# Bucketed attention and two MLPs on one core: the product with v of the first batch goes behind the scores of six steps later

## The chip, the cores and the metric

One core of a Trainium2 chip runs the whole program in one launch. The metric is the device time of one execution in microseconds. Each kernel is timed several times and the median is given. The engines named below are PE (TensorE, matmuls; PEld is its weight load), DVE (VectorE), ACT (ScalarE), POOL (GpSimd) and SP (SyncE, whose queue issues nearly all DMAs here).

## What is computed

Attention over 2 batches of 8 heads, 768 positions, head dimension 64. A query sees only the keys with the same six sign bits. Then two MLPs (512 to 2048 to 512) run over the 1536 rows of 512.

```python
q_bits = (np.einsum('bhsd,dk->bhsk', q, proj) > 0)   # the same for k; bucket = the six bits as a number
scores = np.where(q_bucket[:, :, :, None] == k_bucket[:, :, None, :], scale * q @ k.T, -1e9)
attn = softmax(scores)                                # exp(scores - max), divided by the sum + 1e-9
x = (attn @ v).transpose(0, 2, 1, 3).reshape(1536, 512)
x = gelu_like(x @ w_in1, 1.702) @ w_out1              # h * sigmoid(1.702 h)
out = gelu_like(x @ w_in2, 1.0) @ w_out2              # h * sigmoid(h)
```

## The kernel before

The attention is cut into 96 steps of 128 query rows: six steps a head, 48 steps (steps 0 to 47) a batch. The heads go in pairs. A step j runs through these functions, each with its own line and engine:

- `scores(j)`: four matmuls on PE (lines 404 and 405, twice each) into one of two PSUM buffers `pss`. The second of each pair adds the mask of the buckets.
- `top(j)`: DVE takes the minimum over the row and copies the scores to SBUF tile `p` (line 422). This frees the PSUM buffer, so scores j+2 wait for top j.
- `exps(j)`: ACT, line 427. `p_high(j)`: the f16 half of p into `hl` (line 436 on DVE or 438 on ACT). `p_low(j)`: POOL subtracts it from p, the rest is the lower f16 half (line 442).
- `p_turn(j)`, at odd j: one DMA transpose on SP (line 448) turns the `hl` of two steps into `pt`. There are two `pt` buffers (`PTB = 2`), each for a pair of steps. So the transpose of the pair m (steps 2m and 2m+1) waits until PE is through with the `pt` of pair m-2.
- `av(j)`: 18 matmuls on PE (lines 460 to 462) multiply `pt` by v into the PSUM tile `pav`. It needs the landed transpose.
- `norm`, after the last step of a head's group: DVE divides by the row sums (lines 472 to 476); after the second head of a pair PE transposes the result (line 488, tile `psx`) and ACT and DVE split it into XH and XL (lines 494, 495), which the first MLP reads.

Beside the steps, `ahead` prepares the next pair of heads: loads of q, k and v on SP (lines 268, 279), splits on DVE and POOL (292, 293), transposes on PE (line 300, tile `pstr`), evictions on ACT (307), moves and mask rows by DMA on SP (316, 347), bits on PE (332).

The loop at line 559 runs batch 0 (steps 0 to 47) and then batch 1. In batch 0 an iteration i traces scores i+2, av i-LAG with LAG = 3, top i+1, norm, ahead, exps i, p_high, p_low and p_turn i-1. In batch 1 the scores are one step ahead instead of two, and chunks of the first MLP are traced between the steps. From the iteration `SWITCH - 1` on, which is the last of the first batch's loop, the MLP's PSUM pool takes the place of the scores' second buffer.

The traced order is not the order on the engines. When the program is built, a planner simulates it and puts each engine's instructions in a fixed order: whenever an engine is free in the simulation, it takes the ready instruction with the lowest priority number, which is the place in the trace less an offset (`SOONER`, by function; in batch 0 `av` and `scores` have none, `norm` has 35, all of `ahead` 100 and its functions more). On the chip each engine then works strictly in that order and waits at an instruction whose semaphores aren't there yet. `tc.issue_after(x)` binds the instructions traced inside it to a place behind x in their engine's order; it adds no semaphore.

Of the kernel before, what the change touches and what calls it, by code (L numbers as in the profile page):

```python
# [21 lines left out]
def tile_lsh_attention_two_mlps(  # L22
# [13 lines left out]
    V, A, G, T, SP = nc.vector, nc.scalar, nc.gpsimd, nc.tensor, nc.sync  # L36

    B, H, S, D = q.shape
# [4 lines left out]
    NC = S // P  # L43
    HS = S // 2
    HC = NC // 2
    HEADS = B * H
# [13 lines left out]
    QSCALE = -1.0 / math.sqrt(D)  # L60
    assert math.frexp(QSCALE)[0] == -0.5
    NBUF = 3
    LAG = 3
    TUL = 1
    MORE = {'aq': 1, 'ak': 1, 'p': 1, 'hl': 1, 'pt': 0}
    PTB = 2
# [12 lines left out]

    SOONER = ({'ahead': 100, 'move': 20, 'load_v': 400, 'evict': 200, 'p_high': 200, 'natural': 800, 'p_turn': 35, 'turn': 100, 'p_low': 75, 'top': 35, 'exps': 75, 'bits': 300, 'norm': 35, 'load': 50, 'signs': 20}, {'scores': 200, 'evict': 50, 'norm': 300, 'av': 400, 'natural': 200, 'gate': 50, 'p_turn': 20, 'load_v': 200, 'load': 20, 'sum': 150, 'move': 20, 'p_high': 150, 'rows': 100, 'p_low': 75, 'bits': 100, 'exps': 20}, {'gate': 300, 'sum': 10, 'weights': 50})  # L80
    RATE = (3.4, 2.85)
    SWITCH = HEADS // 2 * NC + LAG + 1
    RING = 3
    RING2 = 6

# [2 lines left out]
    def sooner(task):  # L88
        n = SOONER[stage[0]].get(task, 0)
        return tc.high_priority(offset=n) if n else nullcontext()  # L90
# [158 lines left out]
    def attention(sp, s1, ps_m, ps_v, ahead_of, setup):  # L249
        nat, st = {}, {}  # L250
# [12 lines left out]
        N = len(steps)  # L263
# [55 lines left out]
        def place(n):  # L319
            return n % (NBUF + 1) if n < H else (n - H) % NBUF  # L320
# [74 lines left out]
        def scores(j):  # L395
            n, c = steps[j]
            aq, ak = st["q", n], st["k", n]
            bq, bk = BQ[place(n)], BK[place(n)]
            ps = ahead_of["pool"].tile([P, 2, 512], F32, tag="s", name="pss")
            lq = aq.rearrange("p a b -> p (a b)")[:, c * P:(c + 1) * P]  # L400
            bq = bq[:, c * P:(c + 1) * P]
            for half in range(2):
                o = ps[:, half, 0:HS]
                T.matmul(o, lhsT=lq, rhs=ak[:, half, :], start=True, stop=False)  # L404
                T.matmul(o, lhsT=bq, rhs=bk[:, half * HS:(half + 1) * HS], start=False, stop=True)  # L405
            st["S", j] = ps[:, :, 0:HS]

        count = {}
# [42 lines left out]
        def av(j):  # L451
            (n, c), g = steps[j], group[j]
            vs, s = st["v", n // 2]
            pt = st.pop(("pt", j))
            if j == g[0]:
                st["av", g] = ps_v.tile([P, 512], F32, tag="av", name="pav")
            o = st["av", g][:, c * (D + 1):(c + 1) * (D + 1)]
            for i in range(NC):
                hv, lv = vs[:, n % 2, i, 0:D + 1], vs[:, n % 2, i, D + 1:]
                T.matmul(o, lhsT=pt[:, i], rhs=hv, start=(i == 0), stop=False)  # L460
                T.matmul(o[:, 0:D], lhsT=pt[:, i], rhs=lv, start=False, stop=False)
                T.matmul(o, lhsT=pt[:, NC + i], rhs=hv, start=False, stop=(i == NC - 1))


        def norm(g):
            n, c0 = steps[g[0]]
            m = len(g)
            pr, j = divmod(n, 2)
            vs, s = st["v", pr]
            y = st.pop(("av", g))[:, 0:NC * (D + 1)].rearrange("p (c d) -> p c d", c=NC)[:, c0:c0 + m]  # L470
            ri = sp.tile([P, NC, 1], F32, tag="ri", name="ri", bufs=1)[:, 0:m]
            V.tensor_scalar(ri, y[:, :, D:D + 1], EPS, s[:, j:j + 1], op0=ALU.add, op1=ALU.mult)
            V.reciprocal(ri, ri)
            if ("x", pr) not in st:
                st["x", pr] = sp.tile([P, NC, 2, D], F32, tag="xn", name="xn", bufs=1)
            V.tensor_tensor(out=st["x", pr][:, c0:c0 + m, j, :], in0=y[:, :, 0:D],
                            in1=ri.to_broadcast([P, m, D]), op=ALU.mult)
            if j == 1:
                halves = range(c0 // HC, (c0 + m) // HC)
                for half in halves:  # L480
                    x_turn(pr, half)
                for half in halves:
                    x_split(pr, half)
# [14 lines left out]
        def ahead(pr, s):  # L498
            a, b = 2 * pr, 2 * pr + 1
            return {  # L500
                -4: [(natural, a, "k")],
                -3: [(turn, a, "k", 0), (load, b, "k")],
                -2: [(evict, a, "k", 0), (turn, a, "k", 1), (natural, a, "q")],
                -1: [(evict, a, "k", 1), (turn, a, "q", 0), (v_max, pr), (load, b, "q")],
                0: [(evict, a, "q", 0), (turn, a, "q", 1), (natural, b, "k"), (move, a, "k")],
                1: [(evict, a, "q", 1), (turn, b, "k", 0), (load, a + 2, "k")],
                2: [(turn, b, "k", 1), (v_spread, pr), (natural, b, "q"), (move, a, "q")],
                3: [(evict, b, "k", 0), (evict, b, "k", 1), (turn, b, "q", 0), (v_scale, pr), (load, a + 2, "q")],
                4: [(evict, b, "q", 0), (turn, b, "q", 1), (v_high, pr, 0), (move, b, "k")],
                5: [(evict, b, "q", 1), (bits, pr, 0), (v_low, pr, 0)],  # L510
                6: [(signs, pr, 0), (bits, pr, 1), (v_high, pr, 1), (move, b, "q")],
                7: [(signs, pr, 1), (rows, pr), (v_low, pr, 1)],
                8: [(load_v, pr + 1)],
            }.get(s, [])

        def run(fs):
            for f, *a in fs:
                with sooner(f.__name__):
                    f(*a)
# [36 lines left out]
            run(ahead(1, s))  # L556


        for lead, first, last in ((2, 0, N // 2), (1, N // 2, N)):
            def at(f, j):  # L560
                if first <= j < last:
                    with sooner(f.__name__):
                        f(j)

            for i in range(first - lead, last + LAG + 1):
                if lead == 2:
                    at(scores, i + 2)
                at(av, i - LAG)
                at(top, i + lead - 1)
                m = i - LAG  # L570
                if first <= m < last and m == group[m][-1]:
                    with sooner("norm"):
                        norm(group[m])
                m = i - 2 * (2 - lead)
                if first <= m < last:
                    pr, s = divmod(m, 2 * NC)
                    with sooner("ahead"):
                        if pr + 1 < HEADS // 2:
                            run(ahead(pr + 1, s))
                        if s >= 2 * NC - 4 and pr + 2 < HEADS // 2:  # L580
                            run(ahead(pr + 2, s - 2 * NC))
                at(exps, i)
                at(p_high, i)
                at(p_low, i)
                at(p_turn, i - TUL)
                yield i
                if lead == 1:
                    at(scores, i + 1)
# [107 lines left out]
    with ExitStack() as es:  # L696
# [9 lines left out]
        for i in attention(sp, s1, ps_m, ps_v, ahead_of, lambda: attention_setup(sp, s1, am, ps_m)):  # L706
            if i == -2:
                for _ in range(EARLY):
                    W.fetch()
            if gen is None and i >= WSTART and i % WEVERY == 0 and W.done < 4:  # L710
                W.step()
            if gen is None and i == SWITCH - 1:
                ps_s.close()
                stage[0] = 1
                ahead_of["lead"] = 1
                ahead_of["more"] = {}
                mb = es.enter_context(tc.tile_pool(name="mlpb", bufs=2))
                ahead_of["pool"] = es.enter_context(tc.tile_pool(name="ps_s1", bufs=1, space=PSUM))
                ps_h = es.enter_context(tc.tile_pool(name="ps_h", bufs=2, space=PSUM))
                gen = mlp(0, [0, 1], [[f, f + 1] for f in range(0, NF, 2)], W, mb, ps_h, True, first1)  # L720
            if gen is not None:
                credit += RATE[i >= 3 * HEADS // 4 * NC]
                while credit >= 1.0:
                    credit -= 1.0
                    next(gen, None)
                    background()
# [41 lines left out]
```

## Time and profile before

| | us |
|---|---|
| median of 3 runs | 835.03 |
| lowest and highest run | 831.97 and 836.65 |
| the profiled execution | 831.93 |
| its span, first to last instruction | 830.1 |
| PE busy (91% of the span) | 753.3 |
| DVE, POOL, ACT busy | 533.9, 442.0, 421.4 |

The times below are from the profiled execution, counted from the start of its span. The first batch's steps run from about 9 us (first scores) to 173 us (last product with v), the second batch's, mixed with the first MLP over the first batch's rows, up to about 415 us, and the rest is the MLPs alone. An idle engine costs nothing by itself. What counts in a stretch is the engine or queue whose waits end last.

### The profile page before, as it was taken

What the parts mean: (1) busy time and instruction counts of PE and PEld (TensorE: products, weight loads), DVE (VectorE), ACT (ScalarE), POOL (GpSimd) and SP (SyncE); (2) the same over time, 40 slices, a digit from 0 to 9 for tenths busy, and PEclk for the clock granted to TensorE, in tenths of its full rate; (3) what the DMA queues carried; (4) which work ended last, traced back from release to release, by engine and by line L of the source; (5) the groups of instructions that cost most, each with busy time, mean ns of one, the idle gap of its engine ahead of it and who ended that gap; (6) DMA issues with size and microseconds to landing.
All of it is one profiled execution on the core that took longest, in us unless ns stands there. A gap on an engine that the chain in (4) does not pass through costs nothing.

```text
span 830.1 us, 13998 instructions
## 1 busy us (share of the span) xinstructions
PE 753.3 (91%) x5384; PEld 692.9 (83%) x5384; DVE 533.9 (64%) x932; ACT 421.4 (51%) x721; POOL 442.0 (53%) x345
## 2 busy tenths in 40 slices
PE   6787787698898998988999999979999999999998
PEld 5677576577797887887999999979999989998996
DVE  8877787988689889779424233899733843422222
ACT  6758656596675666655534232444645433321220
POOL 5656676777777857766733242549534533421120
PEclk9778979599999999999999999999999999999999
DMA  4999999998998979865587421232310400000112
GB/s 117 190 180 193 200 180 223 231 247 238 246 254 231 223 216 226 210 153 109 108 300 261 150 104 49 77 127 95 108 51 21 132 2 1 0 1 1 39 39 76
DMA packets 196270, 116.40 MB, mean 140 GB/s; under 512 B 153318, under 2 KB 175846, under 8 KB 196204
## 3 DMA queue, kind: packets, MB, share of 16 engines
q1 hardware_dynamic: 196044, 115.52, 55.8%
q8 instruction: 42, 0.69, 0.3%
q14 instruction: 24, 0.20, 0.1%
q10 hardware_dynamic: 160, 0.00, 0.0%
HBM read 56.63 MB, written 16.78 MB: 88 GB/s over the span
## 4 chain that ended last, share of the span: by engine, by line
PE 59%; DVE 20%; DMA 10%; ACT 5%; issue 4%; POOL 1%; SPq 1%; DVEq 0%; ACTq 0%; POOLq 0%
PE pso L642 26%; PE psh L608 25%; DMA pt<-hl 6%; DVE f L173 3%; DVE p L422 3%; DVE f L171 3%; DVE f L175 2%; DVE f L172 2%; PE pss L404 2%; PE pss L405 1%; PE psbit L332 1%; POOL hl L442 1%; DMA nk<-in_k_dram 1%; PE pav L460 1%; ACT p L427 1%
## 5 line engine op out<-in xcount | busy, mean ns | idle before, releaser
L619 POOL TENSOR_TENSOR gl<-g,gh 128x384 fp32r<-128x384 f32 x128 | 138.3, 1081 | 201.7 <-ACT gh L618 189.5
L442 POOL TENSOR_TENSOR hl<-p,hl 128x768 f16<-128x768 f32 x96 | 168.0, 1757 | 75.7 <-ACT hl L438 33.2
L608 PE MATMUL psh<-XH,wih 128*128 128x384 f32 x512 | 174.2, 340 | 6.0 <-DVE part L651 3.9
L608 PE MATMUL psh<-XH,wil 128*128 128x384 f32 x512 | 173.0, 338 | 0.0
L608 PE MATMUL psh<-XL,wih 128*128 128x384 f32 x512 | 172.9, 338 | 0.0
L617 DVE TENSOR_TENSOR g<-g,psh 128x384 f32<-128x384 f32 x96 | 52.7, 550 | 116.8 <-ACT g L616 116.7
L651 DVE SCALAR_TENSOR_TENSOR part<-pso,part 128x384 f32<-128x384 f32 (+1 forms) x124 | 72.6, 590 | 83.0 <-PE pso L642 82.8
L427 ACT ACTIVATE p<-p,lo 128x768 f32<-128x768 f32 x96 | 89.7, 937 | 70.4 <-DVE p L422 70.2
L618 ACT CAST gh<-g 128x384 fp32r<-128x384 f32 x128 | 65.5, 512 | 86.7 <-DVE g L617 70.7
L608 PEld LDWEIGHTS psh<-XH,wih 128*128 128x128 f32 x512 | 97.2, 190 | 8.1 <-DVE g L614 2.2
L642 PE MATMUL pso<-gh,woh 128*128 128x384 f32 x256 | 88.6, 352 | 16.9 <-DVE g L614 7.0
L422 DVE TENSOR_SCALAR_CACHE_REDUCE p<-pss 128x768 f32<-128x768 f32 x96 | 90.8, 947 | 14.9 <-PE pss L405 8.6
L608 PEld LDWEIGHTS psh<-XL,wih 128*128 128x128 f32 x512 | 97.2, 190 | 0.6
L608 PEld LDWEIGHTS psh<-XH,wil 128*128 128x128 f32 x512 | 97.2, 190 | 0.0
L616 ACT ACTIVATE g<-psh 128x384 f32<-128x384 f32 x96 | 46.8, 488 | 96.2 <-PE psh L608 95.2
L404 PE MATMUL pss<-ak,aq 128*128 128x384 f32 x192 | 77.4, 404 | 19.7 <-DVE p L422 19.5
L642 PE MATMUL pso<-gl,woh 128*128 128x384 f32 x256 | 86.5, 338 | 0.0
L642 PE MATMUL pso<-gh,wol 128*128 128x384 f32 x256 | 86.5, 338 | 0.0
L460 PE MATMUL pav<-VS,pt 128*128 128x65 f16 x576 | 69.4, 205 | 15.4 <-DMA pt<-hl 13.0
L460 PEld LDWEIGHTS <-pt 128*128 128x128 f16 x576 | 57.4, 105 | 24.1 <-DMA pt<-hl 17.7
L642 PE MATMUL pso<-woh,gh 128*128 128x512 f32 x192 | 74.9, 390 | 0.2 <-ACT gh L618 0.2
L642 PE MATMUL pso<-wol,gh 128*128 128x512 f32 x192 | 75.0, 391 | 0.0
(114 smaller groups left out, 1623.1 us busy)
## 6 DMA issues: line engine op xcount, KB each, us to landing
raw<-in_moe_w_in_dram SPq DMA_DIRECT2D x32, 512.0 KB
raw<-in_moe_w_out_dram SPq DMA_DIRECT2D x32, 512.0 KB
spih<-wih SPq DMA_DIRECT2D x13, 256.0 KB
spil<-wil SPq DMA_DIRECT2D x13, 256.0 KB
spoh<-woh SPq DMA_DIRECT2D x13, 256.0 KB
spol<-wol SPq DMA_DIRECT2D x13, 256.0 KB
wih<-spih SPq DMA_DIRECT2D x13, 256.0 KB
wil<-spil SPq DMA_DIRECT2D x13, 256.0 KB
```

The source lines that it names most:

```text
L404: T.matmul(o, lhsT=lq, rhs=ak[:, half, :], start=True, stop=False)
L422: V.tensor_scalar(p, st.pop(("S", j)), LOW, None, op0=ALU.min, op1=ALU.min, accum_out=lo)
L427: A.activation(p, p, AF.Exp, bias=lo, scale=-1.0)
L442: G.tensor_tensor(out=hl[:, 1], in0=st.pop(("p", j))[0], in1=hl[:, 0], op=ALU.subtract)
L460: T.matmul(o, lhsT=pt[:, i], rhs=hv, start=(i == 0), stop=False)
L608: T.matmul(h, lhsT=a[:, c], rhs=x[t][:, c], start=(n == 0), stop=(n == 3 * NDC - 1))
L616: A.activation(g, h, AF.Sigmoid, scale=beta)
L617: V.tensor_tensor(out=g, in0=g, in1=h, op=ALU.mult)
L618: A.copy(gh[:, f], g)
L619: G.tensor_tensor(out=gl[:, f], in0=g, in1=gh[:, f].bitcast(F32), op=ALU.subtract)
L642: T.matmul(y, lhsT=a, rhs=x, start=(n == 0), stop=(n == 3 * nf - 1))
L651: V.scalar_tensor_tensor(out=acc, in0=y, scalar=scale, in1=acc, op0=ALU.mult, op1=ALU.add)
```

## The change

`LAG` becomes a pair, 4 for the first batch and 3 for the second, so that in batch 0 `av(j)` and the norm behind it are traced one iteration later. `SWITCH` moves with it by one, and so stays at the last iteration of the first batch's loop. `scores` keeps its last matmul under `st["did", j]`. In batch 0 the 18 matmuls of `av(j)` are traced inside `tc.issue_after` of the last matmul of scores j+6. Steps 42 to 47 have no scores j+6 yet when they are traced, and are not bound; nor is batch 1.

```diff
-    LAG = 3
+    LAGS = (4, 3)
...
-    SWITCH = HEADS // 2 * NC + LAG + 1
+    SWITCH = HEADS // 2 * NC + LAGS[0] + 1
...
-                T.matmul(o, lhsT=bq, rhs=bk[:, half * HS:(half + 1) * HS], start=False, stop=True)
+                st["did", j] = T.matmul(o, lhsT=bq, rhs=bk[:, half * HS:(half + 1) * HS], start=False, stop=True).ins
...
-            for i in range(NC):
-                hv, lv = vs[:, n % 2, i, 0:D + 1], vs[:, n % 2, i, D + 1:]
-                T.matmul(o, lhsT=pt[:, i], rhs=hv, start=(i == 0), stop=False)
-                T.matmul(o[:, 0:D], lhsT=pt[:, i], rhs=lv, start=False, stop=False)
-                T.matmul(o, lhsT=pt[:, NC + i], rhs=hv, start=False, stop=(i == NC - 1))
+            first = st.get(("did", j + 6)) if j < N // 2 else None
+            with tc.issue_after(first) if first is not None else nullcontext():
+                for i in range(NC):
+                    hv, lv = vs[:, n % 2, i, 0:D + 1], vs[:, n % 2, i, D + 1:]
+                    T.matmul(o, lhsT=pt[:, i], rhs=hv, start=(i == 0), stop=False)
+                    T.matmul(o[:, 0:D], lhsT=pt[:, i], rhs=lv, start=False, stop=False)
+                    T.matmul(o, lhsT=pt[:, NC + i], rhs=hv, start=False, stop=(i == NC - 1))
...
-        for lead, first, last in ((2, 0, N // 2), (1, N // 2, N)):
+        for lead, first, last, LAG in ((2, 0, N // 2, LAGS[0]), (1, N // 2, N, LAGS[1])):
```

## Rows read from the trace of the kernel before

**Rows 1.** Windows by stage: length, busy time of each engine (instructions), PE clock, DMA share.

```profile
20.00:44.00 24.00, 16.89 (x162) 14.85 (x163) 18.91 (x35) 16.48 (x25) 15.24 (x11) 0.74 0.92 188
44.00:154.00 110.00, 86.87 (x974) 74.88 (x971) 89.78 (x167) 74.75 (x108) 71.23 (x45) 0.84 1.01 195
168.00:415.00 247.00, 219.90 (x1934) 201.54 (x1933) 202.34 (x352) 161.48 (x267) 173.08 (x124) 0.97 0.85 205
```

**Rows 2.** SP's issues by line, 65.8 to 132.9 us: ns minimum/median/maximum, first and last start.

```profile
L448 SPq DMA_TRANSPOSE pt<-hl x12: 3580/4179/4519, 65.8 to 128.6; - x12
L347 SPq DMA_DIRECT2D BK<-mk x4: 743/796/852, 70.7 to 106.6; - x4
L347 SPq DMA_DIRECT2D BQ<-mk x4: 743/768/887, 71.6 to 107.3; - x4
L268 SPq DMA_DIRECT2D nq<-in_q_dram x4: 328/516/518, 74.1 to 118.2; - x4
L268 SPq DMA_DIRECT2D nk<-in_k_dram x3: 573/576/576, 78.8 to 113.5; - x3
L279 SPq DMA_DIRECT2D nv<-in_v_dram x2: 385/454/523, 70.1 to 104.4; - x2
L316 SPq DMA_DIRECT2D BQ<-aq x4: 523/592/596, 89.0 to 132.2; - x4
```

**Rows 3.** SP's waits, 44 to 154 us: in total, times, longest.

```profile
SPq L448 <- POOL hl L442: 49.5, 18, 3.8
...
SPq L268 <- DVE sq L293: 2.2, 1, 2.2
...
SPq L448 <- PE pav L462: 0.6, 2, 0.3
```

**Rows 4.** SP's timeline around 50 us and from 109 us: start, duration, issue.

```profile
50.40 0.33 SPq L268 DMA_DIRECT2D nq<-in_q_dram  x1
...
109.00 4.48 SPq L448 DMA_TRANSPOSE pt<-hl  x1
...
114.21 3.89 SPq L448 DMA_TRANSPOSE pt<-hl  x1
...
118.89 4.21 SPq L448 DMA_TRANSPOSE pt<-hl  x1
```

**Rows 5.** POOL's `p_low` counted to 109.05 us: ns minimum/median/maximum, first and last start.

```profile
L442 POOL TENSOR_TENSOR hl<-p,hl x32: 1641/1658/1972, 17.1 to 107.4; 128x768 f16<-128x768 f32 x32
```

**Rows 6.** PE's waits, 20 to 160 us: in total, times, longest.

```profile
PE pss L404 <- DVE p L422: 13.9, 15, 3.4
PE pav L460 <- DMA pt<-hl: 9.6, 6, 3.6
```

**Rows 7.** PE's last matmuls of scores and of av, counted to 42.71 and to 140.63 us.

```profile
L405 PE MATMUL pss<-BK,BQ x22: 336/340/648, 11.8 to 38.5; 128*128 128x384 f32 x22
L462 PE MATMUL pav<-VS,pt x24: 191/192/246, 30.0 to 37.6; 128*128 128x65 f16 x24
...
L405 PE MATMUL pss<-BK,BQ x92: 333/338/648, 11.8 to 136.1; 128*128 128x384 f32 x92
L462 PE MATMUL pav<-VS,pt x228: 190/193/278, 30.0 to 137.7; 128*128 128x65 f16 x114
```

**Rows 8.** PE's timeline at two waits before av: start, duration, [idle before <-releaser].

```profile
42.72 0.24 PE L460 MATMUL pav<-VS,pt 128*128 128x65 f16 x1 [3.64 <-DMA pt<-hl]
...
45.12 0.67 PE L404 MATMUL pss<-ak,aq 128*128 128x384 f32 x1
...
47.02 0.52 PE L404 MATMUL pss<-ak,aq 128*128 128x384 f32 x1
...
115.40 0.20 PE L460 MATMUL pav<-VS,pt 128*128 128x65 f16 x1 [1.70 <-DMA pt<-hl]
...
116.77 0.19 PE L462 MATMUL pav<-VS,pt 128*128 128x65 f16 x1
```

**Rows 9.** ACT's and DVE's timelines behind the wait at 42.72 us.

```profile
44.72 0.49 ACT L307 ACTIVATE aq<-pstr 128x384 fp32r<-128x384 f32 x1 [3.44 <-PE pstr L300]
...
44.95 0.95 DVE L364 TENSOR_REDUCE am<-nv 128x2 f32<-128x768 f32 x1 [4.21 <-DMA nv<-in_v_dram]
```

## The prediction

> **What bounds the kernel now.** I read four views in this order. The windows by stage come first, to find what is scarce in the first batch, the only place that the change binds. From 44 to 154 us no compute engine is full: DVE is busy 89.78 of 110 us, PE 86.87, ACT 74.75, POOL 71.23, while the DMA share is 1.01 [rows 1]. In the second batch PE has 219.90 of 247 us and the DMA share falls to 0.85.
>
> Then SP's issues, because all of that DMA traffic is issued by one queue. Between the transpose at 65.84 and the one at 132.98, 67.1 us in which two pairs of heads (12 pairs of steps) go by, SP issues 12 transposes of 4.18 us, 8 mask rows of 0.78, 4 + 3 loads of q and k of 0.52 and 0.58, 2 loads of v of 0.45 and 4 moves of 0.59: 50.2 + 6.3 + 2.1 + 1.7 + 0.9 + 2.4 = 63.6 us [rows 2]. So SP is 95% occupied and the pace of a pair of steps, 67.1 / 12 = 5.6 us, is SP's pace.
>
> Third, whether the 4.18 us hide a wait. The view of SP's waits gives 49.5 us to POOL's p_low [rows 3], and this is not to be believed: POOL had finished 32 p_lows (steps 0 to 31) by 109.1 us [rows 5], so both steps of pair 15 were there, and its transpose at 114.21 still took 3.89 us [rows 4]. The view names a later count of the same semaphore. The length is the issue itself. What is left of real waiting on SP from 44 to 154 us is 2.2 us once for a split of q, and 0.6 us in two waits for PE's av, which holds the `pt` buffer [rows 3].
>
> Fourth, PE's waits. Before av PE waits 9.6 us in six places for a landing transpose, and 13.9 us before scores for top [rows 6]. These are the waits that the change can touch. They lie on an engine that has 23 us to spare in that stretch.
>
> **The change part by part.** The sum is made against the profiled execution, 831.93 us (span 830.1 and 1.8 around it). The median of the runs is 835.03, 3.1 above it, and the forecast is moved by that.
>
> *The edge.* It adds no instruction and no semaphore, only an order. 42 steps get it. Does it bind? By 42.71 us PE has run 22 / 2 = 11 scores (0 to 10) and 24 / 6 = 4 avs; the next is av 4, behind scores 10, which is j+6 already. By 140.63 us it has run 46 scores (0 to 45) and 38 avs, so av 38 stands behind scores j+7 [rows 7]. Steady state fulfils the edge as it is. One step that doesn't is av 5, which runs on to 45.1 us, with scores 11 right after it [rows 8]. There scores 11 go ahead. They take about 1.9 us (45.12 to 47.02), so av 5 ends that much later; the next user of its buffer is the transpose behind 50.40 us on SP [rows 4], so this is hidden with 3 us to spare, and would cost 1.9 without that cover. Scores 11 come up to 1.4 us earlier. Bounds -1.4 to +1.9; I take 0, since the transpose behind 50 us is the next thing that could be late.
>
> *One iteration later in the trace.* `av` has no offset, so its number rises by what an iteration traces. It changes the order only where av and other work are ready at the same time in the planner's simulation: transposes of the next heads, x_turn, a score. Each such swap puts work into one of the six waits. At most all 9.6 us go and lie on the path; at least nothing. Where did such a wait reach SP? The longest, 3.64 us before 42.72 [rows 8], held back a transpose for ACT, which idled 3.44 us to 44.72; but DVE in that time idled 4.21 us for the load of v, to 44.95 [rows 9], and the split of q that SP then waits 2.2 us for is DVE's. So PE's wait was 0.2 us from being covered by DVE's. I take -0.5, nearest to that row, with -9.6 as the far end. If the wait goes, next late is the load of v for DVE, and behind it SP itself.
>
> *Later av holds `pt` longer.* What is queued behind a late av on PE is scores, and behind the `pt` buffer SP's whole queue, loads and mask rows too. The transpose at 109.00 was landed and used at 115.40, 6.40 us on, and the two avs took to 116.96, 1.56 us [rows 4, 8]. The transpose after next, which needs that buffer, was issued at 118.89: 1.93 us to spare. Below that a later av costs 0; bounds 0 and +7 (worked out in the third rival); I take 0, because the order that av has now already satisfies the edge. A rule of the Trainium skill speaks against the change at this point: "Perfetto Trace Analysis", section "Optimization Strategy", says that the same gap repeating on an engine can mean too few buffers for the next tile. The two `pt` buffers would then be what PE's gaps come from, and holding them longer would make it worse; by that rule the sum would be the third rival's, by the row of 1.93 us to spare it stays at 0.
>
> *The norm one iteration later, SWITCH, second batch.* The switch stays at the loop's last iteration, so nothing is added there. The norm is short DVE work behind av. The rest of the plan is remade: PE idles 27.1 us of 247 in the second batch [rows 1], and I allow a tenth of it in both directions, 2.7 us, with 0 taken.
>
> Sum: 831.93 + 0 - 0.5 + 0 + 0 = 831.4, on the median 834.5 us.
>
> **The rivals.**
> - *The waits before av are worth their length.* Scores and transposes slip into them, tops start sooner, and SP gets its hl and free buffers earlier. For it: six waits, 9.6 us, and a clock of 0.84 in that stretch, a mean over its two levels (1.2 and 2.4 GHz). Against it: SP has only 67.1 - 63.6 = 3.5 us in 67 free. Whole: 835.0 - 9.6 = 825.4; half: 830.2.
> - *It does nothing.* All edges but one are fulfilled and the planner chooses as before: 835.0.
> - *SP comes to wait for PE.* Place: the wait ahead of each transpose for the av of the pair before last, now 0.6 us in total. If av moves behind one more step of work, 5.6 / 2 = 2.8 us, it passes the 1.93 us by 0.87 for every second transpose. Per pair of heads four of six transposes follow without mask rows between them: 1.7 us, over four pairs 7 us: 842. The point from which it decides is a delay of 1.93 us behind the landing.
>
> **How the numbers follow.** About 0.5%, 4.2 us, is what a measurement of this kernel tells from no change: faster is below 830.9, slower above 839.2. Forecast and "does nothing" lie in between: 0.27 and 0.14, together 0.41; the forecast's own range is 831 to 839. The waits paid back, from half of them to all: 0.34, since the row of SP speaks against more than that but the new plan of the second batch can add its 2.7. SP waiting: 0.25. The range of 825 to 842 reaches to the whole of both rivals and leaves out some 2 in 10.
>
> **What would show it.** In the changed kernel's profile: SP's issues from 65 to 133 us still about 63 us of the same 67; SP's wait for av under 2 us in all (the third rival: over 5); PE's waits before av for the landing shorter than 9.6 us, and that time turning up as waits before scores; av 5 behind scores 11, the others behind j+7 or j+8. The last av of step 47 should end within 2 us of 173 us. Wrong it would be if the first batch ends more than 4 us earlier or later, or if it ends the same and the second batch moves.

## The result, and the profile after

The changed kernel takes 840.84 us in the median of 6 runs (836.71 to 842.67), the kernel before 834.70 in 6 runs beside it (831.97 to 836.65). The ratio (over the runs; it is not simply that of the two medians) is 1.0067, with a 95% interval of 1.0042 to 1.0093, so the change costs 0.4 to 0.9%. A second series, with its own runs of the kernel before, gave 1.0101 [1.0068, 1.0133]. The profiled execution of the changed kernel took 840.05 us with a span of 838.3, against 831.93 and 830.1 before: 8.2 us of span to explain. The line numbers of the changed kernel are one higher up to `p_turn` (449), and four higher from `av`'s matmuls (464 to 466) on.

Begin with the first batch, the only part whose trace the change edits. This is the view of windows by stage of the changed kernel; it answers to [rows 1].

```profile
20.00:44.00 24.00, 17.73 (x163) 15.34 (x164) 18.65 (x36) 17.42 (x26) 14.53 (x10) 0.81 0.89 190
44.00:154.00 110.00, 82.14 (x975) 71.92 (x973) 86.54 (x173) 74.52 (x108) 72.95 (x46) 0.89 1.00 200
168.00:415.00 247.00, 217.38 (x1885) 200.20 (x1885) 205.31 (x345) 161.58 (x266) 167.42 (x121) 0.97 0.83 200
```

From 44 to 154 us the work is the same (975 matmuls on PE against 974) and the DMA share is 1.00 again. SP's issues by line over the same twelve pairs of steps as [rows 2], which here begin at 64.42 and end at 135.31:

```profile
L449 SPq DMA_TRANSPOSE pt<-hl x12: 3631/4075/4816, 64.4 to 128.6; - x12
L348 SPq DMA_DIRECT2D BQ<-mk x4: 743/816/835, 68.9 to 105.6; - x4
L348 SPq DMA_DIRECT2D BK<-mk x4: 747/852/1160, 69.8 to 127.6; - x4
L317 SPq DMA_DIRECT2D BQ<-aq x4: 517/524/543, 77.5 to 122.8; - x4
L269 SPq DMA_DIRECT2D nq<-in_q_dram x4: 340/526/580, 71.7 to 116.2; - x4
L269 SPq DMA_DIRECT2D nk<-in_k_dram x4: 500/542/577, 76.9 to 117.4; - x4
L280 SPq DMA_DIRECT2D nv<-in_v_dram x3: 384/586/586, 68.2 to 134.8; - x3
```

With their durations summed, and one load of weights of 0.59 us, that is 64.7 us of issuing in 70.9, or 91%, against 62.6 in 67.1, or 93%, counted in the same way before. SP is as full as it was, the twelve pairs end 2.3 us later than before, and this is made good by the end of the batch: the last product with v of step 47, counted on its last line from 165 to 176 us, ends at 172.8 + 0.2 before and at 172.4 + 0.2 after. First the kernel before, then the changed one:

```profile
L462 PE MATMUL pav<-VS,pt x24: 191/192/196, 166.0 to 172.8; 128*128 128x65 f16 x24
```

```profile
L466 PE MATMUL pav<-VS,pt x12: 191/192/197, 171.4 to 172.4; 128*128 128x65 f16 x12
```

So the whole 8.2 us comes after the first batch, where the source of the program is as before. The next view is windows again, now cut at two milestones: the end of step 47, and the first MLP matmul that needs the second batch's result. The MLP over the first batch has 768 matmuls, which are mixed with the second batch's steps; number 769 starts at 421.42 us before and at 427.25 after. Before:

```profile
173.00:421.40 248.40, 221.38 (x1914) 203.15 (x1914) 201.65 (x354) 160.78 (x269) 173.75 (x126) 0.97 0.84 201
421.40:830.10 408.70, 400.32 (x2112) 376.19 (x2112) 189.81 (x292) 146.18 (x286) 156.82 (x138) 1.00 0.24 81
```

After, with two short windows at the seam between batch 2 and the MLP over it:

```profile
172.60:427.30 254.70, 221.82 (x1911) 204.38 (x1910) 206.73 (x351) 162.26 (x268) 173.82 (x127) 0.96 0.80 193
420.50:427.20 6.70, 2.35 (x40) 1.74 (x39) 1.86 (x5) 1.16 (x3) 2.54 (x3) 0.75 0.30 58
427.20:430.30 3.10, 3.05 (x10) 3.05 (x10) 0.00 (x0) 0.00 (x0) 0.00 (x0) 0.50 0.69 224
427.30:838.30 411.00, 402.80 (x2112) 378.96 (x2112) 188.88 (x292) 146.12 (x285) 155.93 (x136) 0.99 0.24 82
```

PE's work up to the second milestone is the same (221.4 and 221.8 us); its idle time grew from 27.0 to 32.9. The seam shows where most of that lies. PE's timeline there, before (start, duration, and in brackets the idle time and its releaser):

```profile
413.77 0.20 PE L460 MATMUL pav<-VS,pt 128*128 128x65 f16 x1 [0.70 <-DMA pt<-hl]
...
414.88 0.42 PE L642 MATMUL pso<-gh,woh 128*128 128x384 f32 x1
...
417.06 0.49 PE L488 MATMUL psx<-ident,xn 128*128 128x128 f32 x3
...
420.34 0.34 PE L642 MATMUL pso<-gh,wol 128*128 128x384 f32 x1
421.42 0.41 PE L608 MATMUL psh<-XH,wih 128*128 128x384 f32 x1 [0.74 <-DVE part L651]
...
423.26 0.33 PE L608 MATMUL psh<-XL,wih 128*128 128x384 f32 x1
```

And after:

```profile
420.23 0.34 PE L646 MATMUL pso<-gh,wol 128*128 128x384 f32 x1
...
422.81 0.20 PE L464 MATMUL pav<-VS,pt 128*128 128x65 f16 x1 [2.24 <-DMA pt<-hl]
...
423.77 0.22 PE L465 MATMUL pav<-VS,pt 128*128 128x64 f16 x1
423.81 0.24 PE L466 MATMUL pav<-VS,pt 128*128 128x65 f16 x1
...
425.22 0.88 PE L492 MATMUL psx<-ident,xn 128*128 128x128 f32 x3 [1.00 <-DVE xn L480]
427.25 0.69 PE L612 MATMUL psh<-XH,wih 128*128 128x384 f32 x1 [1.16 <-DVE XL L499]
427.74 0.52 PE L612 MATMUL psh<-XL,wih 128*128 128x384 f32 x1
...
430.62 0.35 PE L612 MATMUL psh<-XL,wih 128*128 128x384 f32 x1
```

Both kernels are through with the 768 MLP matmuls at about 420.6 us. Before, 30 of them stand *behind* the last product with v (414.88 to 420.7), and PE works on them while the transpose, the norm and the eviction of the last head run their course. After, all 768 stand *ahead* of it. The last step comes 9 us later (424.2 against 415.1), and PE idles through its landing, its norm and its eviction (2.24 + 1.00 + 1.16 = 4.4 us). Within the last product with v, at 423.8 us, its matmuls go from 0.19 to 0.24 us, and the granted clock is 0.50, the lower level (1.2 GHz), when the MLP goes on: the eleventh matmul from there starts 3.4 us behind the first (427.25 to 430.62), where in the kernel before it starts 1.8 us behind (421.42 to 423.26).

The account of the 8.2 us: first batch -0.4; idle ahead of 420.6 us +2.3 (5.9 - 3.6); idle at the seam +3.6 (4.35 - 0.74); PE busy +0.4 (the transposes at the lower clock); the MLPs from 427.25 us on +2.3 (411.0 - 408.7). Of these 2.3, 1.6 us are lost in the first forty matmuls, at the lower clock. The other 0.7 are lost between 557 and 571 us, where the second MLP begins; this is nothing of the change, since the kernel with the later trace alone, below, lost them in one profiled execution and not in the other. So some two thirds, 3.6 + 0.4 + 1.6 = 5.6 us, belong to the seam.

The part ahead of the seam looks like this in the changed kernel. PE's timeline, the waits at 197 and 224 us:

```profile
197.03 0.45 PE L612 MATMUL psh<-XH,wih 128*128 128x384 f32 x1 [2.62 <-DVE g L618]
...
223.58 0.69 PE L646 MATMUL pso<-gh,woh 128*128 128x384 f32 x1 [2.59 <-DVE part L655]
```

DVE's timeline ahead of the second of them:

```profile
219.22 0.68 DVE L176 SCALAR_TENSOR_TENSOR f<-raw,f 128x512 int32<-128x512 int32 x1
219.82 0.41 DVE L172 TENSOR_SCALAR f<-f 128x512 f32<-128x512 f32 x1
220.27 1.12 DVE L173 TENSOR_SCALAR f<-f 128x512 int32<-128x512 int32 x1
221.42 1.63 DVE L174 SCALAR_TENSOR_TENSOR f<-raw,f 128x512 int32<-128x512 int32 x1
222.98 0.54 DVE L655 SCALAR_TENSOR_TENSOR part<-pso,part 128x384 f32<-128x384 f32 x1
```

The sum that PE waits for stands in DVE's fixed order behind four operations that convert weights; no engine shows a wait for their results from 218 to 230 us. The kernel before has waits of the same kind (`pso` and `psh` behind DVE, 16.8 us in all from 173 to 421 us); after, those are 14.1, but the waits for a landing transpose rose from 3.4 to 8.1 (2.2 of them at the seam), and those before scores from 4.3 to 6.1.

### The profile page after: what moved, and what is told of

Its sections match the earlier page's. It is cut to its first block, busy times and chain, and to the rows that moved or that the text cites. A ratio compares the mean times of both kernels' runs of the same rounds, so it can differ in the third digit from the quotient of the medians.

```text
span 838.3 us, 13997 instructions
## 1 busy us (share of the span) xinstructions
PE 753.0 (90%) x5384; PEld 694.0 (83%) x5384; DVE 531.2 (63%) x932; ACT 423.4 (51%) x721; POOL 441.2 (53%) x345
## 4 chain that ended last, share of the span: by engine, by line
PE 61%; DVE 15%; DMA 10%; issue 5%; ACT 4%; POOL 3%; SPq 2%; ACTq 0%; DVEq 0%; POOLq 0%
PE psh L612 27%; PE pso L646 26%; DMA pt<-hl 8%; DVE p L423 3%; DVE f L174 2%; DVE f L176 2%; PE pss L405 2%; DVE f L172 2%; POOL hl L443 1%; PE pss L406 1%; DVE f L173 1%; DMA nk<-in_k_dram 1%; ACT p L428 1%; SPq L449 1%; PE pav L464 1%
## 5 line engine op out<-in xcount | busy, mean ns | idle before, releaser
L623 POOL TENSOR_TENSOR gl<-g,gh 128x384 fp32r<-128x384 f32 x128 | 141.4, 1106 | 207.6 <-ACT gh L622 195.4
L464 PE MATMUL pav<-VS,pt 128*128 128x65 f16 x576 | 65.6, 200 | 28.1 <-DMA pt<-hl 27.1
L464 PEld LDWEIGHTS <-pt 128*128 128x128 f16 x576 | 54.9, 101 | 38.7 <-DMA pt<-hl 32.1
```

The lines of the kernel that those rows point to most:

```text
L623: G.tensor_tensor(out=gl[:, f], in0=g, in1=gh[:, f].bitcast(F32), op=ALU.subtract)
```

## The experiments

The order in which each engine worked can be laid beside that of the kernel before, trace by trace. To turn one order into the other, at least 933 of PE's 5,384 matmuls have to change places, and 263 of 935 instructions on DVE, 159 of 726 on ACT, 68 of 353 on POOL, 73 of 318 on SP. The first difference on PE is the one forecast, scores 11 (42.41 to 43.82 us) ahead of av 5, in PE's timeline of the changed kernel:

```profile
41.23 0.20 PE L464 MATMUL pav<-VS,pt 128*128 128x65 f16 x1 [2.98 <-DMA pt<-hl]
...
42.41 0.65 PE L405 MATMUL pss<-ak,aq 128*128 128x384 f32 x1
...
43.82 0.28 PE L464 MATMUL pav<-VS,pt 128*128 128x65 f16 x1
```

The wait ahead of av 4 is 2.98 us where it was 3.64 [rows 8]. Most of the others, 781 of the 933, lie in the second batch: with that batch's order bound to the one before, as below, 140 are left on PE. So theory A was: the time is lost by the order that the planner remade for the second batch; the first batch of the change is worth nothing. Its rivals: B, the held-back products with v cost something themselves; C, SP comes to wait for `pt` in the first batch; L, the loss grows with the steps that are traced later. All ratios are to the kernel before on the same chip.

**The later trace without the edge.**

```diff
-            first = st.get(("did", j + 6)) if j < N // 2 else None
+            first = None
```

> Lag 4 in the first batch, without any edge. Theory A (the loss is the remade order of the second batch, which the later trace alone brings; the order of this kernel differs from the changed one on PE alone, at two avs): 839 to 842 us, ratio to before 1.004 to 1.010, the last av of step 95 at 423 to 425 us as in the changed kernel. Rival B (the edges hold av back and that costs the time): 834 to 836, ratio 0.998 to 1.002.

840.99 us, 1.0101 [1.0077, 1.0125]. Its order differs from the changed kernel's at two products with v on PE (steps 5 and 15) and nowhere else. Run again beside the changed kernel itself:

> Lag 4 without the edges, again. Edges worth nothing: ratio to before 1.006 to 1.011, within 0.3% of the changed kernel's. Edges worth something: 1.009 to 1.012 with the changed kernel 0.3 to 0.6% below.

> The changed kernel, beside the one with the lag alone on the same chip. If the edges are worth nothing (they move two avs, 5 and 15, in an order that is otherwise the same): both within 0.3% of each other, ratio to before 1.006 to 1.011. If they gain what they were put in for: this one lower by 0.3 to 0.6%.

841.36 us without the edge and 840.47 with it, 1.0112 [1.0083, 1.0140] and 1.0101 [1.0068, 1.0133]. The two differ by 0.1%, within the intervals; the loss comes with `LAGS`.

**Each half of the plan by itself.** The program is built twice. The first build gives the order of the one kernel; in the second, what is traced from the switch on (the second batch and the MLPs) is bound on each engine to that order, with ordering edges that add no semaphore.

```diff
             if gen is None and i == SWITCH - 1:
+                MARK[0] = len(tc.nc.cur_bb.bb.instructions)
...
+    _, order = build(((3, 3), 0))
+    nc, got = build(((4, 3), 6), order)
...
+                for p, n in zip(places, places[1:]):
+                    tc.add_manual_dep(late[e][n], late[e][p].name,
+                                      _mybir.DependencyInfo(_mybir.DependencyClass.NoSync, _mybir.DependencyReason.DATA),
+                                      reason="pin")
```

The change's first batch with the rest of the kernel before:

> The changed kernel's first batch; from the switch to the second batch on, every engine's instructions traced there are bound to the order that they have in the kernel before. Theory A: the loss is gone, ratio 0.997 to 1.003 (832 to 837 us), last av of step 47 at 171 to 174 us and of step 95 at 414 to 417 us. Rival B (the first batch itself, or what it leaves behind, costs 6 us): ratio 1.004 to 1.010.

The first batch of before with the change's rest (the two builds exchanged):

> The other way round: the first batch of the kernel before, from the switch on the order of the changed kernel. Theory A: ratio 1.004 to 1.010 (838 to 843 us), with step 95's av at 422 to 426 us and PE idle some 6 to 9 us between 415 and 440 us. Rival B: ratio 0.997 to 1.003, step 95's av at 414 to 417.

The first takes 832.82 us against 832.49, 1.0001 [0.9985, 1.0018]: the first batch of the change costs and gives nothing. The second takes 844.72, 1.0142 [1.0115, 1.0168], more than the 1.004 to 1.010 expected: the loss goes with the rest. A is shown, and B and C fall, as far as 0.2% can tell. The seam goes with it. PE's timeline in the first of them:

```profile
414.59 0.20 PE L468 MATMUL pav<-VS,pt 128*128 128x65 f16 x1 [0.69 <-DMA pt<-hl]
...
422.27 0.41 PE L616 MATMUL psh<-XH,wih 128*128 128x384 f32 x1 [0.74 <-DVE part L659]
```

And in the second:

```profile
427.90 0.20 PE L468 MATMUL pav<-VS,pt 128*128 128x65 f16 x1 [2.24 <-DMA pt<-hl]
...
430.18 0.88 PE L496 MATMUL psx<-ident,xn 128*128 128x128 f32 x3 [1.01 <-DVE xn L484]
432.22 0.69 PE L616 MATMUL psh<-XH,wih 128*128 128x384 f32 x1 [1.16 <-DVE XL L503]
```

The second's last product with v of step 47 ends at 178.7 us, 5.7 later than before, while from there to the end of step 95 it takes 250.5 us (the changed kernel 251.6, the kernel before 242.1). So it is 5 us behind the changed kernel, and not by the second batch. That these are paid at the joint of two orders that weren't made for each other is likely but not shown; its 1.4% are in any case not all due to the remade order.

**How much of the later trace it takes.** Lag 4 for the first head alone, without edges:

```diff
-                at(av, i - LAG)
+                now = [j for j in (i - 4, i - 3) if i - j == (4 if lead == 2 and 0 <= j < 6 else 3)]
+                for j in now:
+                    at(av, j)
```

> Lag 4 for steps 0 to 5 alone, no edge: one swap around av 5 at 42 us. Theory A: one swap is enough to remake the whole plan, the first batch still ends at 171 to 175 us (SP's pace), and the time moves by the new order of the second batch alone, to anywhere from 0.99 to 1.012 of before. Rival B: six steps of 48 can't cost more than an eighth of 6 us: 0.998 to 1.002. A third theory (C: the av that is late holds SP's queue by its pt buffer): SP's wait for av grows by the microseconds that the kernel loses.

839.78 us, 1.0094 [1.0069, 1.0118]: six steps traced later cost as much as 48. The traces say why. From the second batch on every engine has the same order as in the changed kernel; 30 matmuls on PE and two instructions on ACT, all in the first batch, would have to change places, and no more. So the one swap at 42 us is enough to bring the whole remade order, and this is the same second batch behind another first one. With lag 4 for steps 0 to 23, and for steps 12 to 47:

> Lag 4 for steps 0 to 23, lag 3 from 24 on, no edge: another plan of the second batch, one that leaves 738 matmuls ahead of the last av. Theory S: near before, ratio 0.998 to 1.005. Theory M: anything from 0.995 to 1.012. That tracing av later is itself what costs (theory L): half of lag 4's loss, 1.003 to 1.006.

> Lag 4 for steps 12 to 47, lag 3 before, no edge; again a plan with 738 matmuls ahead of the last av. Theory S: 0.998 to 1.005. Theory M: anything from 0.995 to 1.012. Theory L: three quarters of the loss, 1.005 to 1.008.

837.65 us, 1.0059 [1.0040, 1.0077], just above what S allowed, and 834.27 us, 1.0039 [1.0017, 1.0062], within it and below what L asked for. For 6, 24, 36 and 48 steps the loss is 0.94, 0.59, 0.39 and 1.01%; it doesn't grow with the steps, and L falls. What these two have that the others lack is the reserve: 30 of the 768 matmuls behind the last product with v, as before, where lag 4 for all steps and for the first head leaves none.

**The reserve at the seam.** Theory S: a good part of the loss is the missing reserve. The changed kernel, with the last 5 of the MLP's 96 pieces (30 matmuls) queued on PE behind the last product with v:

```diff
-                    next(gen, None)
+                    if served < 96 - 5:
+                        next(gen, None)
+                        served += 1
...
+        for _ in range(96 - served):
+            with tc.issue_after(last_av[0]):
+                next(gen, None)
+            background()
```

> The changed kernel, with the last five chunks (30 matmuls, 5.2 us) of the interleaved MLP queued on PE behind the last av of step 95, so that 738 of the 768 interleaved matmuls stand ahead of it as in the kernel before (in the changed kernel all 768 do). Theory S (about half of the loss is the seam: PE idles 4.4 us there instead of 1.4 and comes out of it at the lower clock, 1.5 us more): 3 to 5 us faster than the changed kernel, ratio to before 1.003 to 1.007, PE idle within 410 to 440 us back under 2.5 us. Theory M (the idle spots in the middle of the second batch make the loss, the seam only shows it): ratio 1.008 to 1.011 as the changed kernel.

And the other way, the kernel before with the product with v of step 95 behind the last of the 768 matmuls:

```diff
+            first = last_pso[0] if j == N - 1 else None
```

> The kernel before, with the av of step 95 alone queued on PE behind the last interleaved MLP matmul, so that all 768 stand ahead of it; the order of all else is nearly as before. Theory S: 3 to 5 us slower, ratio 1.0035 to 1.0065. Theory M: ratio 0.998 to 1.002.

835.12 us, 1.0033 [1.0017, 1.0049], and 835.00 us, 1.0044 [1.0023, 1.0064]; the kernel before took 831.40. With the reserve 0.33% is left of the change's 0.67 and 1.01%, and its lack costs the kernel before 3.6 us. So S holds both ways, for half of the loss or somewhat more, with two limits. The first kernel's order differs from the changed one's in more than the 30 matmuls: from 335 us on 213 matmuls on PE and 59 instructions on DVE stand elsewhere. In the second 21 matmuls moved and 10 instructions on DVE and ACT, all behind 414 us, so this one is the cleaner test. PE's timeline at the seam of the changed kernel with a reserve:

```profile
418.27 0.20 PE L465 MATMUL pav<-VS,pt 128*128 128x65 f16 x1 [1.31 <-DMA pt<-hl]
...
421.56 0.49 PE L493 MATMUL psx<-ident,xn 128*128 128x128 f32 x3
...
425.92 0.41 PE L613 MATMUL psh<-XH,wih 128*128 128x384 f32 x1 [0.74 <-DVE part L656]
```

The seam is that of before, full clock included; the 4.5 us by which it comes later (425.9 against 421.4) are what is left in this execution. What the reserve saved is not mainly idle time. From the end of step 47 to matmul 769 PE idles 27.0 us before, 32.9 in the changed kernel and still 31.7 here: most of what left the seam came back between the steps. The larger part of the gain in the traces, 2.4 of 3.7 us, lies behind matmul 769 (408.6 us against 411.0): 1.6 by the clock, which stayed full, and 0.7 in the stretch from 557 us that isn't the change's. And at the seam of the kernel before without one:

```profile
420.71 0.52 PE L493 MATMUL psx<-ident,xn 128*128 128x128 f32 x3 [1.01 <-DVE xn L481]
422.39 0.44 PE L613 MATMUL psh<-XH,wih 128*128 128x384 f32 x1 [1.16 <-DVE XL L500]
```

Two of the three waits are there, and the transposes keep the full clock. This execution, at 833.37 us, is 1.6 below that kernel's median, and its span is 1.5 us longer than that of the kernel before. So the trace shows 1.5 of the 3.6 us; what its slower executions lose more is not shown.

**More of a reserve.** The kernel before with 10 pieces (72 matmuls) behind the last product with v:

> The kernel before with ten chunks queued behind the last av instead of the five that its plan leaves: 696 of 768 matmuls ahead of it, 72 (12.5 us) behind. Theory S says that a reserve beyond the seam's length is worth nothing: PE idles 1.4 us there as it is; ratio 0.998 to 1.002. If attention gains from the room on PE: 0.994 to 0.998; if PE then lacks work in the middle: above 1.002.

841.00 us, 1.0109 [1.0084, 1.0133], and here the expectation was wrong: it cost more than the lack of a reserve. The matmuls held back are missed ahead of the last step, where PE then has nothing between two products with v:

```profile
413.14 0.24 PE L465 MATMUL pav<-VS,pt 128*128 128x65 f16 x1 [5.35 <-DMA pt<-hl]
...
415.11 0.67 PE L613 MATMUL psh<-XH,wih 128*128 128x384 f32 x1
415.57 0.52 PE L613 MATMUL psh<-XL,wih 128*128 128x384 f32 x1
```

The last step ends at 415.3 us, no earlier than before (415.1), though PE idles 32.1 us on the way from step 47 instead of 26.3: the steps, not PE, set that time, so PE's work has to be spread between them.

**DVE's order in the second batch.** Theory G: the other half is what DVE does ahead of the sums that PE waits for. The kernel with the reserve, with the MLP's functions on DVE and ACT moved up in priority:

```diff
-'gate': 50,
+'gate': 150,
...
-'sum': 150,
+'sum': 250,
```

> The changed kernel with the reserve of 30 matmuls, and in the second batch gate at 150 instead of 50 and sum at 250 instead of 150, so that DVE takes the MLP's evictions before the conversion of weights. Theory G (what is left of the loss, 3 to 4 us, is PE waiting for DVE behind those conversions, as the 2.6 us at 223 us in the changed kernel): ratio 0.997 to 1.001. Otherwise 1.003 or more.

834.77 us, 1.0038 [1.0022, 1.0054], against 835.12 and 1.0033 without it. This does not test G. In the two traces every engine has its instructions in the same order: the new offsets changed no decision of the planner, DVE's order stayed as it was, and the run is the kernel with the reserve once more. The two ratios agree, as they should, and whether DVE's order makes what is left of the loss stays open.

**Other remade plans.** Theory P: the planner's constants belong to the order of before, and any edit that remakes it loses. Two edits leave the trace as it was and change one offset of the first batch in `SOONER`:

```diff
-'turn': 100,
+'turn': 60,
```

> The kernel before (lag 3, no edge) with the offset of turn in the first batch 60 instead of 100: a change of the first batch that has nothing to do with av, and that remakes the plan with all 768 matmuls ahead of the last av. Theory P (before's order of the second batch is a good one that its constants belong to; any remade one is worse, most of all one without a reserve): ratio 1.005 to 1.013. Theory L (tracing av later is what costs): 0.997 to 1.003.

```diff
-{'ahead': 100,
+{'ahead': 60,
```

> The kernel before (lag 3, no edge) with the offset of ahead in the first batch 60 instead of 100: again a remade plan, this one with 738 matmuls ahead of the last av. Theory P: 1.002 to 1.007, as the lag-4 plans with a reserve. Theory L: 0.997 to 1.003.

839.99 us, 1.0085 [1.0064, 1.0106], without a reserve at the seam, and 836.47, 1.0054 [1.0036, 1.0073], with 30 matmuls. Neither traces a product with v later. Seven kernels whose order the planner made anew, unforced (the change, lag 4 without edges, three lags by part, two offsets), were measured, and all were slower by 0.4 to 1.1%. Three of them (the change, lag 4 without edges and for the first head) share one order of the second batch, so these are five different ones. They fall into two groups by the seam:

| behind the last product with v | kernels | ratio to before |
|---|---|---|
| 30 matmuls | lag 4 to step 23, from step 12; `ahead` 60 | 1.0059, 1.0039, 1.0054 |
| none | the change, lag 4 without edges, for the first head; `turn` 60 | 1.0067 and 1.0101, 1.0101 and 1.0112, 1.0094, 1.0085 |

P holds for these five orders. That *any* other plan loses is not shown, and no version that was run beats the kernel before.

## Why the prediction was wrong

The forecast was 834.5 us and no change; measured were 840.84, and slower by 0.67%. Slower had 0.25. That 840.84 lies inside the range of 825 to 842 is luck: the upper end is the price of a rival that didn't come.

- *SP sets the pace of the first batch.* Right. Summed by single durations instead of medians SP issued for 62.6 of 67.1 us, 93% and not 95%; in the changed kernel for 64.7 of 70.9. And no wait of SP for the product with v appears in its view from 44 to 154 us there (0.6 us in [rows 3]).
- *The edge binds only at av 5, and costs nothing.* Right but for a second place, av 15, as laying the order without the edge beside that with it shows. The medians with and without the edge differ by 0.1%, less than their intervals. The others were forecast behind scores j+7 or j+8; of the 42 bound steps 20 stand behind j+6, 19 behind j+7 and 3 behind j+8.
- *One iteration later, -0.5.* The term is near enough: the first batch ended 0.4 us earlier, and alone it is worth 1.0001. Its working went the other way. The waits before av were to shrink from 9.6 us and those before scores to grow; this is PE's view of waits from 20 to 160 us:

```profile
PE pav L464 <- DMA pt<-hl: 18.9, 11, 3.0
PE pss L405 <- DVE p L423: 8.6, 8, 2.0
```

Those before av doubled and those before scores fell from 13.9 [rows 6]. The order on PE shows why: av is traced later, but the planner placed it earlier. In the kernel before the av of the first 42 steps stand behind scores j+7.1 on average, 32 of them behind j+7 or later; in the changed kernel behind j+6.6, and 22 of them behind j+7 or later. PE comes to av with fewer scores done and waits there for the landing. So the title says where the edge lets av stand at the earliest, and not that av moved back. This cost nothing, as the kernel with this first batch and the rest of before shows (1.0001).

- *Later av holds `pt`.* 0, as taken. The rival built on it, at 842 us, came closest to the measured time and was still wrong: its wait didn't appear. The rule that had been put beside it ("Perfetto Trace Analysis" of the Trainium skill, section "Optimization Strategy": the same gap repeating on the engine that should be saturated can mean too little room for the next tile) doesn't bear on PE, which isn't the full one there (busy for 82 of 110 us, SP for 91%). The changed kernel's trace shows no such shortage either: PE's gaps before av grew from 9.6 to 18.9 us and SP didn't wait for a buffer.
- *"The rest of the plan is remade: PE idles 27.1 us of 247 in the second batch [rows 1], and I allow a tenth of it in both directions, 2.7 us, with 0 taken."* **This is the step that failed.** The term measured +6 us in the medians and +8.6 in the profiled execution, and no row stood behind the choice of a tenth. It had the wrong place, the wrong size and the wrong centre. The place: a tenth of the idle time between 168 and 415 us leaves out the seam at 415 to 421, where PE's 5.6 busy us in the window of 6.3 were cover, 30 matmuls in the timeline at the seam that nothing required to stand there. The centre: the order of before is one of many that the planner can make, and the five others that were made all lost 0.4 to 1.1%, so a remade plan was no even bet.

The prediction's own test named this case: wrong "if it ends the same and the second batch moves". The first batch ends 0.4 us from where it did, and the second batch moved.

What stays open: the loss ahead of the seam (0.33% with the reserve restored, 3.7 us in the medians). The waits of PE there are spread over `pt`, the scores, and DVE's sums. The one cause that was to be tried, DVE's order, was not: the edit left it as it was.

## What to carry to other kernels

Where a planner fixes each engine's order for the whole program, an edit in one stage can be an edit in all of them: compare the built orders before the edit is priced, and bind the order of the rest to the old one when the edit's own worth is wanted. Compare them before an experiment is believed, too: an offset that changes no place tests nothing, and six steps traced later can bring the same order as 48. At a seam where the next stage needs the last result of this one, count the independent work that stands behind the last step: here 30 matmuls of 0.17 us covered a landing, a norm and an eviction, to leave none there cost 3.6 us, and 72 cost 8.5.

## What the runs showed of the hardware

In the changed kernel TensorE's granted clock fell to 0.50, the level of 1.2 GHz, at 423.8 us, within the last product with v. Ahead of that the engine had idled 2.24 us, to 422.8, and then worked for 1 us; two more waits, 1.00 and 1.16 us, came at the lower level. The next forty matmuls took 8.6 us, against 7.0 before. In all six profiled executions without a reserve whose order the planner made (the change and lag 4 without edges, twice each, lag 4 for the first head, `turn` 60) the waits are 2.2 to 2.3, 1.0 and 1.2 us, and those forty matmuls take 8.5 to 9.9 us. In all that have the 30 matmuls they take 7.0, and so they do in the kernel before without its reserve, where the waits are 0.7, 1.0 and 1.2 us and the clock stayed full.
